# Two small reads placed second on the load queues of a fused attention and mixer kernel

## The chip, the cores and the metric

The kernel runs on one core of one Trainium2 chip. The metric is the device time of one execution in microseconds (us). Engines are named as in the profile: PE (TensorE, matmuls), PEld (its weight loads), DVE (VectorE), ACT (ScalarE), POOL (GpSimd) and SP (SyncE, which here only issues transfers). Transfers run on the core's 16 DMA engines; SP and ACT each have a queue of their own to them, and a transfer of either brings sixteen completion counts in the trace.

## The reference: what is computed

Input x has 2048 rows (tokens) of 640 bf16 numbers. Two branches work on it and a gate mixes them:

```
g = sigmoid((x * gate_w).sum(-1))
a = linear_attention(x, wqkv) @ wo      # q, k, v = x @ wqkv; 32 heads of 20; phi(q), phi(k);
                                        # kv = phi(k)^T v, z = sum phi(k); o = phi(q) kv / (phi(q) z)
h  = gelu(layernorm(x) @ w1); x1 = x + shifted(h) @ w2
b  = x1 + gelu(layernorm(x1) @ w3) @ w4
out = g * a + (1 - g) * b
```

phi(t) is t + 1 where t is positive and exp(t) elsewhere, plus 1e-6. wqkv is 640 x 1920: columns 0 to 640 are wq, the next 640 wk, the last wv.

## The kernel before

The tokens are cut into 16 tiles of 128 rows, and the 640 input columns into 5 slices of 128, so a product with wq is five matmuls that add up in one PSUM bank. All of x, q, k and the activations stay in on-chip memory. The work runs in stages: q and k of every tile (to about 54 us), then the sums over tokens that the attention needs and the first layernorm (to 78 us), w1 and w2, w3, and at the end w4 together with the attention's output, tile by tile, with the gate and the store.

What matters here is the first 10 us. All loads are issued at the start, in the order in which L716 to L739 write them, on two queues. `load_x(t)` (L702) loads x tile t, 128 rows of 1,280 bytes, on SP's queue. `load_wq(k, queue)` (L705) loads slice k of wq, its first 512 columns: 128 rows of 1,024 bytes that lie 3,840 bytes apart. `load_wk` (L708) does the same for wk, in the same 3,840-byte rows. The last 128 columns of wq come in a load of their own (L729). By queue the order is:

- SP: x tile 0, x tile 1, wq slice 2, x tile 2, wk slices 0 and 2, x tile 3, wk slice 4, x tile 4, and then turns of x tiles and further loads;
- ACT: wq slices 0, 1, 3 and 4, wk slices 1 and 3, the rest of wq;
- POOL: the gate's weights, 1,280 bytes (L734).

All of these are recorded on one line of the helper, L285. The turns (`x_turn`, L711, L281 in the profile) turn x tiles 3 to 15 from rows to columns by DMA. Tiles 0, 1 and 2 are turned on PE instead (`t_x`, L798; the transposes have L637), copied from PSUM to xT by DVE (L691) and used at once.

PE begins with matmuls on constants (`warmup`, L904) that fill the time until x tile 0 is there. `q_three` (L949) then writes the order of the first q products by hand, as pairs (tile, slice), where (1, None) and (2, None) are the transposes of that tile:

```
order = [(0, 0), (1, None), (0, 1), (1, 0), (1, 1), (0, 2), (1, 2), (0, 3), (1, 3), (2, None), (0, 4), (1, 4),
         (2, 0), (2, 1), (2, 2), (2, 3), (2, 4)]
```

The products are recorded on L942 (`stream`). `k_two` (L958) follows with k of tiles 0 and 1. `k_out` (L954) evacuates a k tile and lets ACT square the x tile into a buffer that nothing reads, `junk`, for the row sums.

Later work isn't in a fixed order: `_Items.run` (L336) picks the next piece of work by times from a clock of its own (`simulate`, L232), which counts 0.5 us for an issue and a fixed rate for bytes. Waits are worked out from the buffers: an instruction that writes what another has written waits for it (`_collect`, L122), and every transfer has a semaphore. `emit` (L296) lets POOL wait for all load semaphores at the end of its program.

Of the kernel before, what the change touches and what calls it, by code (L numbers as in the profile page):

```python
# [11 lines left out]
D = 640  # L12
# [404 lines left out]
def _build(nc, A_x, A_wqkv, A_wo, B_w1, B_w2, B_w3, B_w4, gate_w, out, dbg=None, stop=None):  # L417
    sch = _Sched(nc)
# [65 lines left out]
    junk = pa.alloc("junk", [128, 1, D], BF16)  # L484
# [94 lines left out]
    def dve(fn, reads, writes, cost=None):  # L579
        if cost is None:  # L580
            n = nfree(writes[0])
            cost = 65.0 + n / 0.96
        return sch.op("dve", fn, reads, writes, cost=cost)
# [113 lines left out]
    x2 = A_x[0]  # L697

    def dma_in(out_ap, in_ap, key, **kw):
        return sch.dma("sp", out_ap, in_ap, key, **kw)  # L700

    def load_x(t):  # L702
        dma_in(x_tok[:, t, :], x2[128 * t:128 * (t + 1), :], "x%d" % t)

    def load_wq(k, queue):  # L705
        sch.dma(queue, wq[:, k, 0:512], A_wqkv[128 * k:128 * (k + 1), 0:512], "wq%d" % k)
# [7 lines left out]
    gwr = xn[:, 1, 0:128]  # L714
    dve(lambda e: e.memset(gwr, 0.0), [], [gwr])
    load_x(0)  # L716
    load_wq(0, "act")
    load_x(1)
    load_wq(1, "act")
    load_wq(2, "sp")  # L720
# [647 lines left out]
    for t in range(NT):  # L1368
        c = t // 4
# [94 lines left out]
def bass_gated_mix__linear_attn_block__mixer_s_mlp__prompt_kernel(  # L1464
    nc, A_x, A_wqkv, A_wo, B_x, B_w1, B_w2, B_w3, B_w4, gate_w, out
):
    assert tuple(A_x.shape) == (1, S, D) and tuple(out.shape) == (1, S, D)
    assert tuple(A_wqkv.shape) == (D, 3 * D) and tuple(A_wo.shape) == (D, D)
    assert tuple(B_w1.shape) == (D, D) and tuple(B_w2.shape) == (D, D)
    assert tuple(B_w3.shape) == (D, F) and tuple(B_w4.shape) == (F, D) and tuple(gate_w.shape) == (D,)  # L1470
    _build(nc, A_x, A_wqkv, A_wo, B_w1, B_w2, B_w3, B_w4, gate_w, out)
# [28 lines left out]
```

## Time and profile before

| what | value |
|---|---|
| three runs | 259.14, 259.16 and 259.90 us; median 259.16 |
| the profiled execution | 259.62 us, of which its span (first to last instruction) 258.4 |
| PE busy | 253.2 us, 98% of the span |
| DVE, ACT, POOL busy | 145.6, 107.0, 90.2 us |
| granted PE clock | 1.00 |
| x tile 0: issue, landing | 0.79, 3.65 us |
| x tile 1: issue, landing | 1.26, 4.33 us |
| wq slice 2: issue, landing | 1.71, 6.17 us |
| wq slice 3: issue, landing | 1.72, 6.37 us |
| x tile 2: issue, landing | 2.18, 7.93 us |
| wq slice 4: issue, landing | 2.20, 8.12 us |

Times of instructions count from the start of the span. A transfer's landing is the moment at which the last of its sixteen completion counts (one from each DMA engine) arrives. In rows of the timeline the columns are the start, the length, the engine, the line, the operation and its output and inputs; what stands in brackets is the idle time of the engine just before, and what ended it. In lists of waits the columns are who waited for whom, the sum in us, the number of waits and the longest. In tables by stage each engine has its busy time and, in brackets, how many instructions; then come the granted clock, the busy share of the DMA engines and GB/s.

### The profile page before, as it was taken

To read this page: it belongs to the slowest core of one execution; us is meant where nothing else is said; L and a number is where in the kernel's file an instruction comes from. 1 tells how busy PE (TensorE), PEld (TensorE's weight loads), DVE (VectorE), ACT (ScalarE), POOL (GpSimd) and SP (SyncE) were. 2 spreads that over 40 slices of the span, in tenths; PEclk is the share of its full clock that TensorE was granted. 3 is DMA by queue.
4 is the path that set the end of the run, shared out by engine and by line. 5 is a ranking of instruction groups with operands and counts; after the bars stand their busy time and mean duration, and the time that the engine had idled before them with its cause. 6 is when DMAs were issued, how large, how long until landed. Compare 5 with 4: busy or idle time off the path is not lost.

```text
span 258.4 us, 3579 instructions
## 1 busy us (share of the span) xinstructions
PE 253.2 (98%) x1392; PEld 110.9 (43%) x1242; DVE 145.6 (56%) x290; ACT 107.0 (41%) x219; POOL 90.2 (35%) x146
## 2 busy tenths in 40 slices
PE   8899999999999999999999999999999999999997
PEld 4333333344444333334444444444444444444444
DVE  2588888899962995489999803759200033200033
ACT  1396776751356757665655600003520100253000
POOL 5012299967772143758918001223000022300000
DMA  6777799555843599462565400032100032200002
GB/s 189 221 176 182 155 142 220 157 125 119 111 102 72 103 321 387 95 103 51 127 104 128 102 10 20 0 127 50 28 0 0 20 23 101 101 1 3 0 20 102
DMA packets 57825, 26.48 MB, mean 103 GB/s; under 512 B 49188, under 2 KB 56397, under 8 KB 57808
## 3 DMA queue, kind: packets, MB, share of 16 engines
q1 hardware_dynamic: 54976, 21.87, 36.1%
q0 software_dynamic: 1168, 3.28, 4.9%
q10 hardware_dynamic: 1664, 1.11, 1.4%
q8 instruction: 10, 0.16, 0.3%
q14 instruction: 7, 0.06, 0.1%
HBM read 12.04 MB, written 2.62 MB: 57 GB/s over the span
## 4 chain that ended last, share of the span: by engine, by line
PE 95%; DMA 2%; issue 1%; SPq 0%; DVE 0%
PE ps L606 37%; PE ps L1237 30%; PE ps L625 13%; PE ps L831 7%; PE ps L614 4%; DMA x_tok<-in_A_x_dram 2%; PE ps L942 1%; PE ps L1283 1%; PE ps L1143 1%; SPq L285 0%; PE ps L1029 0%; DVE Mt L691 0%; PE ps L637 0%; PE ps L1055 0%; DVE x_tok L665 0%
## 5 line engine op out<-in xcount | busy, mean ns | idle before, releaser
L606 PE MATMUL ps<-xnT,w 128*128 128x512 bf16 x352 | 79.9, 379 | 0.5 <-issue 0.2
L665 DVE SCALAR_TENSOR_TENSOR x_tok<-ps,stg,abx 128x512 bf16<-128x512 f32 (+2 forms) x17 | 12.2, 719 | 78.4 <-PE ps L1237 78.3
L682 ACT ACTIVATE h2T<-ps 128x512 bf16<-128x512 f32 x52 | 30.7, 596 | 59.8 <-PE ps L606 59.8
L606 PEld LDWEIGHTS ps<-xnT,w 128*128 128x128 bf16 x360 | 34.6, 98 | 41.5 <-issue 2.1
L1237 PE MATMUL ps<-w,h2T 128*128 128x512 bf16 (+2 forms) x218 | 45.9, 366 | 0.3 <-issue 0.2
L648 POOL TENSOR_SCALAR xn<-x_tok,st 128x640 bf16<-128x640 bf16 x32 | 34.2, 1076 | 25.8 <-DMA xnT<-xn 25.3
L648 POOL TENSOR_SCALAR abx<-x_tok,stg 128x640 f32<-128x640 bf16 (+1 forms) x16 | 14.8, 934 | 72.1 <-DVE x_tok L665 72.1
L1237 PEld LDWEIGHTS ps<-w,h2T 128*128 128x128 bf16 x221 | 21.1, 98 | 24.2 <-issue 0.3
L682 ACT ACTIVATE Er<-ps 128x512 bf16<-128x512 f32 (+1 forms) x36 | 23.0, 648 | 15.5 <-PE ps L614 10.6
L681 ACT ACTIVATE junk<-x_tok 128x640 bf16<-128x640 bf16 x32 | 23.6, 738 | 3.9 <-DVE x_tok L663 3.7
L682 ACT ACTIVATE hsT<-ps 128x512 bf16<-128x512 f32 (+1 forms) x32 | 19.0, 593 | 13.5 <-PE ps L606 13.2
L625 PE MATMUL ps<-w,hsT 128*128 128x512 bf16 x76 | 22.3, 379 | 0.0
L625 PE MATMUL ps<-wkg,xT 128*128 128x512 bf16 x67 | 20.1, 379 | 0.1
L663 DVE SCALAR_TENSOR_TENSOR x_tok<-ps,x_tok 128x640 bf16<-128x640 f32 x16 | 13.1, 820 | 10.8 <-PE ps L614 10.2
L1237 PE MATMUL ps<-M_sb,pqnT 128*128 128x512 bf16 (+2 forms) x83 | 18.7, 366 | 0.1
L614 PE MATMUL ps<-wkg,xT 128*128 128x130 bf16 x80 | 17.6, 220 | 0.2
L831 PE MATMUL ps<-pk_tok,x_tok 128*128 128x512 bf16 x79 | 17.7, 379 | 0.1
L614 PE MATMUL ps<-w,hsT 128*128 128x128 bf16 x80 | 17.5, 219 | 0.2
L1172 DVE TENSOR_TENSOR pq_tok<-pq_tok,dnr 128x300 bf16<-128x300 bf16 (+1 forms) x48 | 17.1, 410 | 0.6
L648 DVE TENSOR_SCALAR Er<-Er 128x512 bf16<-128x512 bf16 (+1 forms) x36 | 12.2, 340 | 6.8 <-ACT Er L682 6.0
L606 PE MATMUL ps<-wq,xT 128*128 128x512 bf16 x64 | 15.9, 379 | 0.0
L656 DVE TENSOR_TENSOR qprod<-qprod,pk_tok 128x640 f32<-128x640 f32 x13 | 15.1, 1164 | 0.4
(90 smaller groups left out, 252.8 us busy)
## 6 DMA issues: line engine op xcount, KB each, us to landing
w<-in_B_w_dram SPq DMA_DIRECT2D x1, 2160.0 KB, 8.1
w<-in_B_w_dram SPq DMA_DIRECT2D x1, 2080.0 KB, 13.0
out_dram<-x_tok SPq DMA_DIRECT2D x3, 640.0 KB, 3.1
w<-in_B_w_dram POOLq DMA_DIRECT2D x8, 160.0 KB, 4.0
x_tok<-in_A_x_dram SPq DMA_DIRECT2D x6, 160.0 KB, 4.4
x_tok<-in_A_x_dram SPq DMA_DIRECT2D x1, 960.0 KB, 5.8
wv<-in_A_wqkv_dram POOLq DMA_DIRECT2D x1, 800.0 KB, 5.5
x_tok<-in_A_x_dram SPq DMA_DIRECT2D x1, 640.0 KB, 4.9
```

Of the source, the lines that this page charges most:

```text
L606: ins = e.matmul(out_ap, l, r, start=(i == 0), stop=(i == n - 1))
L614: return e.add_instruction(mybir.InstMatmult(name=nc.get_next_instruction_name(), engine=e.engine, ins=[e.lower_ap(r), ll], outs=[e.lower_ ...
L625: e.matmul(outs[0], l, r, start=st, stop=sp, skip_group_check=True)
L648: return engf(lambda e: e.tensor_scalar(out_ap, in_ap, s1, s2, op0, op1), rd, [out_ap], cost=cost)
L656: return engf(lambda e: e.tensor_tensor(out_ap, a, b_, op), [a, b_], [out_ap], cost=cost)
L663: return dve(lambda e: e.scalar_tensor_tensor(out_ap, in0, scalar, in1, op0, op1, accum_out=accum), rd, [out_ap, accum], cost=cost + 70.0)
L665: return dve(lambda e: e.scalar_tensor_tensor(out_ap, in0, scalar, in1, op0, op1), rd, [out_ap], cost=cost)
L681: return act(lambda e: e.activation(out_ap, in_ap, func, bias=bias, scale=scale, accum_out=accum), rd, wr, cost=cost)
L682: return act(lambda e: e.activation(out_ap, in_ap, func, bias=bias, scale=scale), rd, wr, cost=cost)
L831: ins = e.matmul(o, l, r, start=(t0 + q_ == 0), stop=(t0 + q_ == NT - 1))
L1172: dve(lambda e, o=o, i0=i0, i1=i1: e.tensor_tensor(o, i0, i1, ALU.mult), [i0, dnr[:, 1, sd, :]], [o], cost=cost)
L1237: ins = e.matmul(o, l, r, start=first and i == 0, stop=last and i == len(prs) - 1, skip_group_check=True)
```

## The change

Two reads are added, and nothing else. Behind x tile 0, SP issues a read of 64 bytes (32 columns) from every eighth row of x tile 2, sixteen rows in all, into 16 partitions of `junk`. Behind wq slice 0, ACT issues a read of 64 bytes from every eighth row of wq slices 1, 2, 3 and 4, sixteen rows of each slice, into the same partitions. Nothing uses the values: the same bytes are loaded again with their tiles and slices. In the words of the change that is 64 bytes of one row for each of the 16 DMA engines. Each read has a semaphore of its own.

```diff
     load_x(0)
+    sch.dma("sp", junk[0:16, 0, 128:160], x2[256:384:8, 0:32], "tx")
     load_wq(0, "act")
+    sch.dma("act", junk[0:16, 0, 0:128].rearrange("p (k c) -> p k c", c=32),
+            A_wqkv[128:D, 0:32].rearrange("(k e r) c -> e k r c", e=16, r=8)[:, :, 0, :], "tw")
     load_x(1)
     load_wq(1, "act")
     load_wq(2, "sp")
```

## The prediction

> **What bounds the kernel now.** The first view is the busy table: PE is busy for 253.2 us of a span of 258.4 us. So the kernel is bound by matmuls, and the only time to be had is where PE stands still. The second view is the list of waits of PE, cut to the first 10 us and then to the rest. The first 10 us hold this:
> ```profile
> PE ps L904 <- PEq L1485: 0.8, 1, 0.8
> PE ps L637 <- DMA x_tok<-in_A_x_dram: 0.7, 1, 0.7
> ```
> The first is the start of the program, before any load. Behind 10 us the list has two waits of 0.2 us and nothing else. So one wait counts, that of the transposes (L637) of x tile 2 for its load. The chain that ended last says the same, and from 8 us to the end it is almost all PE:
> ```profile
> 1.71 0.43 SPq L285
> 2.14 0.04 issue
> 2.18 5.75 DMA x_tok<-in_A_x_dram
> 7.93 0.05 issue
> 7.98 0.45 PE ps L637 x5
> ```
> Tile 2 is the fourth load on SP's queue, issued at 2.18, and lands 5.75 us later at 7.93. The timeline of PE and of its weight loads around it shows how much time stands open:
> ```profile
> 5.21 2.04 PE L942 MATMUL ps<-wq,xT 128*128 128x512 bf16 x7
> 7.98 0.45 PE L637 MATMUL ps<-ident,x_tok 128*128 128x128 bf16 x5 [0.73 <-DMA x_tok<-in_A_x_dram]
> ...
> 5.75 0.10 PEld L942 LDWEIGHTS ps<-wq,xT 128*128 128x128 bf16 x1 [0.29 <-DVE xT L691]
> 6.21 0.55 PEld L942 LDWEIGHTS ps<-wq,xT 128*128 128x128 bf16 x4 [0.36 <-DMA wq<-in_A_wqkv_dram]
> ```
> Matmuls of 512 columns overlap: two in a row start 0.216 us apart (five take 1.08 in the chain) though each lasts 0.379. The last of the seven ends at 7.25, so it starts at 6.87 and the next could start at 7.09: open until 7.98 are 0.89 us. The matmul of 5.75 could be followed at 5.97 and is followed at 6.21, when wq slice 2 is there: 0.24 us more. **The ceiling of any gain here is 0.89 + 0.24 = 1.13 us**, since behind 8 us PE runs without a gap.
>
> Why does tile 2 land late? The table by stage of the first loads (DMA share and GB/s are the last two columns) tells where its 5.75 us go:
> ```profile
> 3.00:4.00 1.00, 1.00 (x9) 0.63 (x8) 0.00 (x0) 0.00 (x0) 0.84 (x4) 1.00 1.00 323
> 4.00:5.00 1.00, 1.00 (x9) 0.69 (x8) 0.65 (x2) 0.85 (x1) 0.71 (x5) 1.00 0.72 224
> 5.00:6.00 1.00, 1.00 (x8) 0.44 (x5) 0.71 (x3) 0.43 (x1) 0.00 (x0) 1.00 0.82 236
> 6.00:7.00 1.00, 0.93 (x5) 0.31 (x4) 0.00 (x0) 0.00 (x0) 0.00 (x0) 1.00 1.03 353
> 7.00:8.00 1.00, 0.27 (x3) 0.02 (x2) 0.00 (x0) 0.00 (x0) 0.00 (x0) 1.00 1.07 383
> ```
> The loads fall from 323 to 224 GB/s while both queues are full, and recover at 6 us. In the trace's packet records nearly all 1,280-byte packets last 0.055 us; between 3.9 and 6.2 us some twenty last 0.2 to 0.69 us, in wq slices 2 to 4 and x tile 2 alone. The slices of wk, which lie in the same rows as wq, follow with none. The sixteen completion counts of tile 2, one per DMA engine, come between 5.44 and 7.93, fifteen of them by 7.00, where x tile 0's spread over 0.6 us. So rows that an engine has not touched before seem to cost it a stall, and tile 2 collects them.
>
> **The change, part by part.** *Issues.* Each of the two queues gets one more issue before its second load: by the rows of the page's own issues 0.40 to 0.46 us on SP and on ScalarE. Everything behind is issued that much later: tile 1 at 1.72 for 1.26, tile 2 at 2.65 for 2.18. Does that move a landing? From 2.3 us to 10 us data is queued, so at best nothing; at worst the whole 0.47 us. I take 0.25 for tile 1, as tile 0's packets last until about 2.8 us and tile 1's would be there some 1.03 us after issue (the lag of tile 0: issue at 0.79, first packet at 1.82), at 2.75 for 2.29; and 0 for what stands behind it. *Bytes.* 16 x 64 and 64 x 64 bytes are 5 KB; one packet on SP's ring and four on ScalarE's for each engine. The nearest row is the 256-byte packet of a transpose, 0.018 us: 5 x 0.018 = 0.09 us, inside the 0.25.
>
> *First touch.* The read of each new region is paid ahead, for all five regions, in 64-byte packets. What is it worth? At the least nothing, where the stall only changes its place. At the most all the stall: 4 to 6 us ran at 224 and 236 GB/s against 368 from 6 to 8 us (mean of 353 and 383), which loses 2 x (1 - 230/368) = 0.75 us on the mean engine, and the last engine is another 0.93 us late (7.00 to 7.93). The mean engine's 7.00 less 0.75 is 6.25; with x tile 0's spread of 0.6 us instead of tile 2's, and tile 1's 0.25, the last count comes by about 6.7. t_x(2) can't start before 7.98 - 1.13 = 6.85. So the load stops being the bound, and the gain is the ceiling less what tile 1 loses, since its transposes (PE at 4.37, landing at 4.33) have no slack: **1.13 - 0.25 = 0.88 us**. Late next are the DVE copies of xT (0.29 and 0.39 us of wait in the timeline), and wq slice 4, needed 0.32 us behind the start of the transposes of tile 2, at 7.3, and landing at 8.12 now, with fifteen counts by 7.26; it is one of the slices touched.
>
> *Edits at nothing.* ScalarE's table load moves from 4.15 to 4.6 and ends at 5.9; its first activation comes at 8.71, or 7.8. SP has nothing to do from 5.46 to 10.20, when it waits for tile 3. Both reads write junk, so ScalarE's first Square (12.91) waits for them; they are there by 5 us, and behind it stand only later activations. POOL gets two waits behind its last work. The order of later work is written by the planner from its own clock: there tile 1 moves from 0.894 to 1.000 us of load start, everything behind it by the same 0.106 us, and PE's wait for the gate row, the last in the planner's start-up, too. Equal shifts change no comparison, so order and banks stay. If they did not, any of the later 250 us could move; I give it no price but the edges of the range.
>
> *Is the gain kept?* PE has no wait for a load behind 8 us. The nearest is wk slice 0: needed at 9.66 - 0.88 = 8.78, landing at 8.71 and, of the same rows, earlier if the stall goes. xT of tile 5 lands at 19.0 for a matmul at 20.74.
>
> *Against the median.* The profiled execution took 259.62 us (span 258.4 and 1.2 around it), the median of three is 259.16, the others 259.14 and 259.90. How much of the 0.46 is this same stall I can't see. 259.62 - 0.88 = 258.74; I take the step, not the level, to the median: **259.16 - 0.88 = 258.3 us**. If the median execution stalls less than the profiled one, by the whole 0.46, the gain is 0.42 and the time 258.7.
>
> **The rivals.** *A: the stall only moves.* The touch stands in each ring ahead of tile 1 and wq slice 1, which wait for it; the later stall shrinks by as much. Tile 2 lands when it does now: 259.1 to 259.2. For it: the load of w3, alone on its queue, starts slowly although five blocks are touched in turn, and needs about 2 us:
> ```profile
> 90.50:91.50 1.00, 1.00 (x9) 0.44 (x5) 0.97 (x3) 0.98 (x3) 0.00 (x0) 1.00 0.62 59
> 91.50:92.50 1.00, 1.00 (x7) 0.31 (x5) 1.00 (x3) 0.03 (x1) 0.00 (x0) 1.00 0.77 218
> 93.50:94.50 1.00, 1.00 (x8) 0.46 (x6) 1.00 (x2) 0.28 (x2) 0.47 (x3) 1.00 1.05 429
> 97.50:98.50 1.00, 1.00 (x8) 0.35 (x4) 0.00 (x0) 0.97 (x2) 1.00 (x2) 1.00 1.06 396
> ```
> Against it: 64-byte reads hold little, and five can be open at once beside tile 0's data.
>
> *B: the stall is not first touch.* The last line above is w4, as new as w3, right behind it on the same queue, and at full rate from its start. So a slow start may belong to an idle queue, and the dip at 4 to 6 us to something else. Then the change brings only later issues: 0 to 0.47 us, 259.2 to 259.6. The Trainium skill, "HBM Reference", Latency, gives a mean access time of 0.2 us and 2 us at high load; by that rule the stalls come from load and a read ahead changes nothing. The trace disagrees as far as it goes: there are none at 383 GB/s and many at 224.
>
> *C: slower.* The touch stalls the rings and spares nothing, as 64 bytes warm only a piece of what an engine reads later (each reads eight rows). Then everything from tile 1 on is late by the stall: w3's longest first packet took 1.07 us, the 960 KB load of x at 22 us 1.51. Nothing covers it, since tile 2's wait is already open: 259.16 + 1.07 = 260.2, up to 260.7. From a stall of 0.78 us that isn't given back it shows as slower.
>
> **How the numbers follow.** A difference of 0.3%, 0.78 us, is about what a measurement of this kernel can tell from no change. The forecast, a gain of 0.4 to 1.13 us, has 0.55: 0.45 above 0.78 us, 0.10 below. A has 0.14 and B 0.13, both within 0.3%; C has 0.18. So faster 0.45, same 0.37, slower 0.18. The range runs from the ceiling, 259.16 - 1.13 = 258.0, less 0.1 for scatter, to B's end, 259.6: it leaves out C. The forecast's own range is 258.0 to 258.8.
>
> **What would show it.** Right: the stretch from 4 to 6 us at over 300 GB/s, long packets gone from wq slices 2 to 4 and tile 2, its landing before 7.1, the wait of L637 gone and tile 1 landing by 4.6. A: long packets in the small reads, tile 1 later by over 0.5 us, tile 2 as now. B: the dip unchanged and every landing up to 0.47 us late. C: tile 2 behind 8.9. The prediction fails if the typical execution has less stall than the profiled one, or if a load behind 8 us becomes a wait of PE.

## The result and the profile after

The changed kernel took 259.65 us (median of 22 runs, 259.19 to 261.63), the kernel before 259.02 us in the same comparison (22 runs, 258.3 to 259.9). The ratio is 1.0029 with a 95% interval of 1.0017 to 1.0040: slower, by 0.29% or some 0.7 us (what an unchanged kernel reads against itself is run 4 below). The forecast was 258.3 us and its range ended at 259.6, so the sign is the other one.

The profiled execution of the changed kernel took 259.44 us, with a span of 258.2. PE's waits in the first 10 us:

```profile
PE ps L907 <- PEq L1488: 0.8, 1, 0.8
PE ps L637 <- DMA x_tok<-in_A_x_dram: 0.5, 1, 0.5
```

The second looks like the wait of before (0.7 us), made shorter. It is another wait of the same line: the timeline shows for which tile. The transposes (L637) of tile 0 stand at 3.66, those of tiles 1 and 2 are these:

```profile
5.45 0.71 PE L637 MATMUL ps<-ident,x_tok 128*128 128x128 bf16 x5 [0.52 <-DMA x_tok<-in_A_x_dram]
5.96 2.00 PE L945 MATMUL ps<-wq,xT 128*128 128x512 bf16 x7
7.79 0.44 PE L637 MATMUL ps<-ident,x_tok 128*128 128x128 bf16 x5
...
9.68 0.38 PE L945 MATMUL ps<-wkg,xT 128*128 128x512 bf16 x1
```

Tile 2 (7.79) follows the matmuls without a wait, as the prediction wanted. Tile 1 now has one: it is turned at 5.45. In the kernel before that is 0.71 us earlier and without a wait:

```profile
4.74 0.63 PE L637 MATMUL ps<-ident,x_tok 128*128 128x128 bf16 x5
```

The chain that ended last runs through its load, which before ran through that of tile 2:

```profile
1.26 0.40 SPq L285
1.67 0.04 issue
1.71 3.70 DMA x_tok<-in_A_x_dram
5.41 0.05 issue
5.45 0.71 PE ps L637 x5
```

The issue at 1.26 is the small read, and tile 1's, behind it, comes at 1.71 for 1.26. Issued 0.45 us later, tile 1 lands 1.08 us later (5.41 for 4.33). The stages of the first loads (the last two columns are DMA share and GB/s):

```profile
3.00:4.00 1.00, 1.00 (x9) 0.68 (x8) 0.00 (x0) 0.00 (x0) 0.82 (x4) 1.00 0.67 159
4.00:5.00 1.00, 0.94 (x6) 0.34 (x4) 0.65 (x2) 0.38 (x1) 0.73 (x5) 1.00 0.93 292
5.00:6.00 1.00, 0.55 (x6) 0.55 (x6) 0.22 (x1) 0.90 (x1) 0.00 (x0) 1.00 1.06 338
```

The dip that stood at 4 to 6 us (224 and 236 GB/s) is gone from there and now stands at 3 to 4 us (159 for 323), one load earlier. The small reads did not pay for it: their packets took 0.011 us each, and the long packets (0.17 to 0.67 us) are now in tile 1's load, which had none.

**One number carries the comparison.** In the profiled execution of every kernel of this study the span is the start of the first k matmul (`ps<-wkg,xT`, 9.68 above) plus 248.5 us, to 0.1 us: 9.88 and 258.4 before, 9.68 and 258.2 after, 8.76 and 257.3 in the fastest. So only what comes before it decides. The reported time is 1.2 to 1.3 us above the span, so by this estimate before's median of 259.02 stands for a first k matmul at about 9.3, and after's 259.65 for one at 9.9. The profiled execution of before, with 9.88, was one of its slowest (259.62 of 258.3 to 259.9).

### The profile page after: what moved, and what is told of

The parts are those of the page before. It is cut to its first block, busy times and chain, and to the rows that moved or that the text cites. A ratio compares the mean times of both kernels' runs of the same rounds, so it can differ in the third digit from the quotient of the medians.

```text
span 258.2 us, 3583 instructions
## 1 busy us (share of the span) xinstructions
PE 253.2 (98%) x1392; PEld 110.8 (43%) x1242; DVE 145.0 (56%) x290; ACT 107.1 (41%) x219; POOL 90.7 (35%) x146
## 4 chain that ended last, share of the span: by engine, by line
PE 96%; DMA 1%; issue 1%; DVE 0%; SPq 0%
PE ps L606 37%; PE ps L1240 30%; PE ps L625 13%; PE ps L834 7%; PE ps L614 4%; PE ps L945 2%; DMA x_tok<-in_A_x_dram 1%; PE ps L1286 1%; PE ps L1146 1%; PE ps L1032 0%; PE ps L637 0%; SPq L285 0%; DVE Mt L691 0%; PE ps L1058 0%; DVE x_tok L665 0%
## 5 line engine op out<-in xcount | busy, mean ns | idle before, releaser
L663 DVE SCALAR_TENSOR_TENSOR x_tok<-ps,x_tok 128x640 bf16<-128x640 f32 x16 | 13.1, 821 | 10.7 <-PE ps L614 10.1
```

Source lines behind the costliest of these rows:

```text
L663: return dve(lambda e: e.scalar_tensor_tensor(out_ap, in0, scalar, in1, op0, op1, accum_out=accum), rd, [out_ap, accum], cost=cost + 70.0)
```

## The experiments

Each kernel ran beside the kernel before on the same chip. All keep the order of work on PE and DVE; the runs with a late issue add memsets on DVE at the start. "Lands" is the last of a load's sixteen counts.

**1. The change with small reads from rows already read**

```diff
-    sch.dma("sp", junk[0:16, 0, 128:160], x2[256:384:8, 0:32], "tx")
+    sch.dma("sp", junk[0:16, 0, 128:160], x2[0:128:8, 0:32], "tx")
-            A_wqkv[128:D, 0:32]...
+            A_wqkv[0:128, 0:128]...        # as many bytes, of slice 0
```

> The change, with its two small reads taken from rows that the loads ahead of them have just read (x tile 0, wq slice 0) and not from new ones: the same issues, the same 80 packets of 64 bytes, no new region touched. Theory 1 (first touch: the small reads pay the stall of new rows ahead of x tile 1): x tile 1 lands by 4.8 us and not at 5.41, x tile 2 at 7.5 to 8.4, the dip of the loads stays at 4 to 6 us; time 259.0 to 259.5. Theory 2 (the dip comes when the gate's small read of the POOL queue gets its turn, which the change moves ahead): as the change, tile 1 at 5.2 to 5.6, dip at 3 to 4 us. Theory 3 (a small transfer between two large ones empties the queue, whatever rows it reads): also as the change, 259.4 to 259.9.

Measured: 259.87 us, ratio 1.0031 (1.0013 to 1.0049). x tile 1 lands at 6.02. The loss is the change's, with nothing touched ahead: which rows the small reads name doesn't matter to it.

**2. Before, with all first loads from the same rows**

```diff
-        dma_in(x_tok[:, t, :], x2[128 * t:128 * (t + 1), :], "x%d" % t)
+        s_ = 0 if t < 3 else t
+        dma_in(x_tok[:, t, :], x2[128 * s_:128 * (s_ + 1), :], "x%d" % t)
-        sch.dma(queue, wq[:, k, 0:512], A_wqkv[128 * k:128 * (k + 1), 0:512], "wq%d" % k)
+        sch.dma(queue, wq[:, k, 0:512], A_wqkv[0:128, 0:512], "wq%d" % k)    # load_wk likewise
```

> The kernel before, with x tiles 1 and 2 read from the rows of tile 0 and with all slices of wq and wk read from the rows of slice 0: as many loads, packets and bytes, but no new rows behind the first load of each queue until x tile 3 (this computes with wrong values). Theory 1 (first touch): the dip at 4 to 6 us goes, x tile 2 lands by 6.8 us, time 0.4 to 1.0 us below before. Theories 2 and 3: the dip stays where it is, x tile 2 at 7 to 8 us, time as before.

Measured: 259.19 us, 0.9998 (0.9986 to 1.0010), with 294 and 291 GB/s at 4 to 6 us and single packets of up to 1.28 us, though the rows were those of the first loads. With run 1 this ends first touch as the cause of the dip.

**3. No gate read (POOL's queue), before and with the change**

```diff
-    sch.dma("pool", xn[0:KD, 1, 0:128], gate_w.rearrange("(k p) -> k p", p=128), "gw")
```

> The kernel before, without the read of the gate's weights on POOL's queue (they stay zero, so this leaves out the gate's sums). Theory 1 (first touch) and theory 3 (the small transfers themselves): the dip at 4 to 6 us stays, x tile 2 lands at 7 to 8 us, time within 0.4 us of before. Theory 2 (the gate's read makes the dip): 4 to 6 us at over 320 GB/s, x tile 2 by 6.8 us, time 0.4 to 1.0 us below before.

> The change, without the read of the gate's weights (they stay zero). Theory 1 and theory 3: as the change, x tile 1 lands at 5.2 to 5.6 us, dip at 3 to 4 us, time 259.4 to 259.9. Theory 2: tile 1 lands by 4.8 us, no dip, x tile 2 by 7 us, time 258.0 to 258.6.

Measured: 259.36 us, 1.0013 (0.9994 to 1.0031), without the read in the kernel before, and the dip stays (279 and 265 GB/s). 259.89 us, 1.0042 (1.0020 to 1.0063), in the changed one: the loss is all there. The small transfer on the third queue is not it.

**4. The kernel before, unchanged**

> The kernel before, unchanged, as a kernel of its own: what no change reads as, and a second trace of it. Its x tile 2 landed at 7.93 us in the first trace, in an execution 0.5 us above the median of 35. If that execution was an unlucky one, tile 2 lands here by 7.3 us and the ratio is within 0.998 to 1.002.

Measured: 259.45 us, 1.0013 (0.9999 to 1.0028). So a ratio of 1.0013, or of 0.9987, reads as no change here. Its trace has 297 and 287 GB/s at 4 to 6 us, x tile 2 at 7.54 and the first k matmul at 9.57. PE waits there for wq slice 2 (0.9 us) and not for tile 2. The dip of 224 and 236 from which the prediction was worked out, and the wait for tile 2, belong to one execution.

**5. Before, with tile 1 and wq slice 1 issued late, and no small reads**

```diff
-    load_x(1)
-    load_wq(1, "act")
+    for _ in range(2):
+        late = dve(lambda e: e.memset(junk[:, 0, :], 0.0), [], [junk[:, 0, :]], cost=230.0)
+    sch.dma("sp", x_tok[:, 1, :], x2[128:256, :], "x1", deps=[late])
+    sch.dma("act", wq[:, 1, 0:512], A_wqkv[128:256, 0:512], "wq1", deps=[late])
```

> The kernel before, with no small reads, but with x tile 1 and wq slice 1 issued 0.45 us later: they wait for two DVE memsets of junk that end about there. Theory 4 (it is the later issue: the data queues run empty behind x tile 0, and a queue that starts anew has slow first packets): x tile 1 lands at 5.2 to 6.0 us, the loads drop below 200 GB/s between 3 and 4 us, time 259.4 to 259.9. Theory 3 (the small transfer itself upsets what follows): tile 1 lands by 4.8 us, time 259.0 to 259.4.

Measured: 259.76 us, 1.0040 (1.0019 to 1.0060). The two are issued at 1.81, 0.1 us later than in the change, and land at 5.97 and 6.16. Its wait of PE for tile 1, and its stages:

```profile
PE ps L637 <- DMA x_tok<-in_A_x_dram: 1.3, 1, 1.3
```

```profile
3.00:4.00 1.00, 1.00 (x9) 0.69 (x8) 0.00 (x0) 0.00 (x0) 0.82 (x4) 1.00 0.78 105
4.00:5.00 1.00, 0.69 (x6) 0.30 (x4) 0.65 (x2) 0.25 (x1) 0.73 (x5) 1.00 0.88 255
5.00:6.00 1.00, 0.00 (x0) 0.00 (x0) 0.00 (x0) 1.00 (x1) 0.00 (x0) 1.00 1.06 368
```

**The whole loss without any small read**, and the dip in the change's place, deeper (105 GB/s). PE does nothing from 5 to 6 us. So the later issue costs, not the transfer that took the place.

**6. The small reads elsewhere in the queues**

Third (behind x tile 1 and wq slice 1), and behind all first loads:

```diff
     load_x(1)
+    sch.dma("sp", junk[0:16, 0, 128:160], x2[256:384:8, 0:32], "tx")
     load_wq(1, "act")
+    sch.dma("act", junk[0:16, 0, 0:128]..., A_wqkv[128:D, 0:32]..., "tw")
```

> The change, with both small reads behind x tile 1 and wq slice 1 and not ahead of them, so that more data is queued ahead when they come. Theory 4: x tile 1 lands at 4.2 to 4.6 as before, the queues don't run empty, x tile 2 at 7 to 8, time 258.9 to 259.4. Theory 3: what follows the reads is upset, wq slice 2 lands by over 0.7 us later than before (6.2), x tile 2 at 8 to 9, time 259.5 to 260.3.

> The change, with both small reads behind all first loads (on SP's queue behind x tile 4, on ACT's behind the rest of wq). Theory 4: no load is issued later, so the time is as before, 258.8 to 259.4, ratio 0.998 to 1.002, and x tile 1 lands at 4.2 to 4.6. Theory 3: the reads themselves cost, over 1.002.

Measured: third 259.48 us, 1.0023 (1.0007 to 1.0038). Tile 1 lands at 4.59, and the dip moves with the reads to 4 to 5 us (164 GB/s). Last 259.12 us, 1.0018 (1.0001 to 1.0035). The medians fall the further back the reads stand, but the intervals overlap, and neither of these two can be told from run 4's 1.0013: the reads' bytes and packets cost nothing that shows. With the reads last the first loads are issued as before, and its trace has 308 and 335 GB/s at 4 to 6 us, no wait of PE for a load, and the first k matmul at 9.38 all the same; run 10 says why.

**7. One part of the change alone, and one queue late alone**

```diff
     load_x(0)
+    sch.dma("sp", junk[0:16, 0, 128:160], x2[256:384:8, 0:32], "tx")     # x read only
```

```diff
     load_wq(0, "act")
+    sch.dma("act", junk[0:16, 0, 0:128]..., A_wqkv[128:D, 0:32]..., "tw")    # wq read only
```

```diff
-    load_x(1)
+    for _ in range(2):
+        late = dve(lambda e: e.memset(junk[:, 0, :], 0.0), [], [junk[:, 0, :]], cost=230.0)
+    sch.dma("sp", x_tok[:, 1, :], x2[128:256, :], "x1", deps=[late])     # tile 1 late only
```

> Of the change only the read of x tile 2 on SP's queue. Theory 4: x tile 1 is still issued 0.45 us late, but ACT's queue goes on with wq slice 1 and hides the gap in part: tile 1 at 4.6 to 5.2 us, time 259.1 to 259.5. Theory 3: one small transfer for each engine is enough, tile 1 at 5.2 to 6.0, time 259.4 to 259.9.

> Of the change only the read of the wq slices, on ACT's queue. Theory 4 (a load issued after the first data moves, at about 1.7 us, starts slowly once what was issued ahead of it is used up): x tile 1 keeps its issue at 1.26 and lands at 4.0 to 4.5 us, wq slice 1 is issued at 1.72 and lands at 5.0 to 6.0 and is what PE waits for; x tile 2 at 6.5 to 7.8; time 259.0 to 259.8. Theory 3 (the small transfer itself): tile 1 is late too, at over 4.8.

> The kernel before, with no small reads, with x tile 1 alone issued 0.45 us later (it waits for two DVE memsets of junk), and all of SP's queue behind it. It is to the run with the x read alone what the late issue of both was to the change. Theory 4: as that run, x tile 1 at 5.8 to 6.5 us, x tile 2 at 8 to 8.8, time 260.2 to 262. Theory 3: tile 1 by 4.8, time 259.0 to 259.5.

Measured: 261.42 us, 1.0087 (1.0055 to 1.0119); 260.52 us, 1.0070 (1.0043 to 1.0096); 260.89 us, 1.0071 (1.0045 to 1.0098). Each half is worse than the whole, which the forecasts of the first two had not (at most 259.9 and 259.8 us). In the two on SP's queue tile 1 lands at 6.24 and 6.80; with the read on ACT's it lands at 4.22, and wq slice 1, now issued at 1.72, at 6.43, for which PE waits 1.6 us. One queue that is late seems to fall behind the other's later loads. Tile 1 late by memsets does what the x read does, without any read. Part of the 261.42 is the clock: four of its seven executions had a mean granted clock of 0.993. Part of tile 1 late alone is PE's pace (run 10 for both).

**8. More bytes issued before the first data**

The loads of wq put together in another way, with x tile 2 as SP's third issue; no small reads:

```diff
-    load_wq(1, "act")
-    load_wq(2, "sp")
-    load_wq(3, "act")
+    sch.dma("act", wq[:, 1:5, 0:512], A_wqkv[128:640, 0:512].rearrange("(k p) f -> p k f", p=128), "wq1")
...
-    load_wq(4, "act")
```

The other two take slices 1+2 and then 3+4 as ACT's second and third, and slices 0+1 and then 2 to 4 as its first and second.

> The kernel before, with wq slices 1 to 4 in one load of 512 KB, second on ACT's queue (issued at 1.24), and x tile 2 third on SP's queue (1.71). Theory 4: more data is issued before the first moves, the rate stays over 320 GB/s from 3 to 6 us, x tile 2 lands by 6.9; but slice 1 comes with slice 4 at 5.4 to 6.2 and PE waits for it; time 258.4 to 259.0. If the dip is a matter of time or of bytes and not of issues, it is at 4 to 6 us as before and the time is 259.0 to 259.8.

> The kernel before, with wq slices 1 and 2 in one load, second on ACT's queue, slices 3 and 4 in one behind it, and x tile 2 third on SP's. Theory 4: the first two issues of each queue carry 720 KB and not 576, so the dip comes later and is shorter: x tile 2 by 7.0, slices 1 and 2 at 4.9 to 5.4 where slice 1 alone is needed at 5.2; time 258.2 to 258.9, below both kernels. If the dip doesn't hang on issues: as before.

> The kernel before, with wq slices 0 and 1 in one load, first on ACT's queue, slices 2 to 4 in one, second, and x tile 2 third on SP's. In all runs so far the span is 248.5 us behind the first k matmul, so only the first 10 us count. Theory 4: as with slices 1 to 4 in one there is no dip from 3 to 5 us, and PE doesn't wait for slice 1: first k matmul at 8.7 to 9.1, time 258.3 to 258.8, below both kernels. If long loads have stalls of their own, as with the pairs (one engine's part of slices 3 and 4 came 3 us late): 259.2 to 261.

Measured: slices 1 to 4 in one 258.99 us, 1.0003 (0.9992 to 1.0014); in pairs 260.78 us, 1.0075 (1.0048 to 1.0101); two and three 258.67 us, 0.9987 (0.9976 to 0.9998). With 960 KB in the first two issues of each queue the dip is gone. The stages of two and three:

```profile
4.00:5.00 1.00, 1.00 (x9) 0.67 (x8) 0.65 (x2) 0.66 (x1) 0.72 (x5) 1.00 1.09 388
5.00:6.00 1.00, 1.00 (x8) 0.49 (x6) 0.71 (x3) 0.00 (x0) 0.00 (x0) 1.00 1.08 386
6.00:7.00 1.00, 1.00 (x8) 0.51 (x7) 0.00 (x0) 0.00 (x0) 0.00 (x0) 1.00 1.06 389
```

PE is busy throughout, tile 2 lands at 6.09, and the first k matmul starts at 8.76:

```profile
6.88 0.44 PE L637 MATMUL ps<-ident,x_tok 128*128 128x128 bf16 x5
...
8.76 0.38 PE L939 MATMUL ps<-wkg,xT 128*128 128x512 bf16 x1
```

**In its trace this version beats both kernels**; by the median it gains 0.13%, no more than run 4's kernel is off from itself. Slices 1 to 4 in one gain nothing, as slice 1 then lands with slice 4 at 5.67 and PE waits 0.5 us for it. The pairs missed their forecast of 258.2 to 258.9: with 704 KB ahead the third issue is slow again (eight counts of slices 3+4 by 5.88, the last at 9.24), and PE waits 3.0 us for them.

**9. The small reads beside the regrouped loads**

```diff
+    sch.dma("act", wq[:, 0:2, 0:512], A_wqkv[0:256, 0:512]..., "wq0")
+    sch.dma("sp", junk[0:16, 0, 128:160], x2[256:384:8, 0:32], "tx")
+    sch.dma("act", junk[0:16, 0, 0:96]..., A_wqkv[256:D, 0:32]..., "tw")
     load_x(1)
+    sch.dma("act", wq[:, 2:5, 0:512], A_wqkv[256:640, 0:512]..., "wq2")
```

and the same with the reads third, behind both.

> The kernel with wq slices 0 and 1 in one load and 2 to 4 in one, and the change's small reads (x tile 2; slices 2 to 4) second on each queue. Theory 4: x tile 1 and slices 2 to 4 are issued at 1.7 and not at 1.25, with only 416 KB ahead of them, so the dip is back between 3 and 5 us: x tile 1 at 5 to 6 us (4.63 without the reads), first k matmul 0.4 to 1.2 us later than 8.76, time 259.0 to 260.0. If the reads only add bytes: 258.6 to 258.9.

> The same regrouped kernel with the small reads third, behind x tile 1 and slices 2 to 4, so with 960 KB queued ahead of all that they delay. Theory 4: no dip, x tile 2 issued at 2.2 and landing at 6.0 to 6.6, time 258.5 to 258.9 as without reads. If a small read costs wherever it stands ahead of needed data: x tile 2 later than 7, time over 259.1.

> The kernel of the run that regrouped wq's loads and kept the small reads second, once more: its executions fell into two groups, five at 258.9 to 259.5 us and seven at 261.3 to 262.7, and its trace was of the fastest one. Theory later issue alone: two groups differ in when x tile 1 or 2 lands, so a trace of a long one shows the first k matmul near 11.5 us (9.12 in the short one) at a clock of 1.00. Theory clock: a trace of a long one shows a granted clock below 1.00 in some slices and a first k matmul at most 1 us later. If the trace falls in the short group again, the median alone is of use: 258.9 to 262.6 us, and what makes the long group stays open.

Measured: third 258.64 us, 0.9999 (0.9979 to 1.0019): behind 960 KB the reads cost nothing that can be seen, though they also bring nothing. Second 261.44 us, 1.0073 (1.0042 to 1.0105), and once more 259.27 us, 1.0009 (0.9982 to 1.0036). Both traces were of short executions (258.85 and 258.68 us; tile 1 at 5.05 and 4.79). The forecast had the dip back between 3 and 5 us, as only 416 KB are queued ahead; neither trace has it (342 and 327 GB/s at 4 to 5 us). Seven of the first twelve executions were over 261.2 us, two of the second over 261.1, and six of these nine had a mean granted clock of 0.993 for 1.000.

**10. PE made to stand still**

```diff
-    load_x(1)
+    for _ in range(12):
+        late = dve(lambda e: e.memset(junk[:, 0, :], 0.0), [], [junk[:, 0, :]], cost=38.0)
+    sch.dma("sp", x_tok[:, 1, :], x2[128:256, :], "x1", deps=[late])
```

> Before, with x tile 1 alone held back by twelve DVE memsets instead of its place in the queue (issue at about 6.4 us by 1.34 + 11 x 0.46), no small reads. It is made to leave PE idle for more than 4 us. In every trace so far the span is the start of the first k matmul plus 248.5 us. Theory clock: the executions that are about 2 us longer, with a mean granted clock of 0.993, are those in which PE stood idle early and its clock was granted lower for a while afterwards; 0.7% of a span of 258 us is 1.8 us. Then this kernel's trace shows a granted clock below 1.00 in some slices behind 5 us, a mean of about 0.99, and a span that is longer than the first k matmul plus 248.5 us, or the first k matmul itself late by more than the load. Rival: PE's clock has nothing to do with its idle time; then every slice shows 1.00 and the span is the first k matmul plus 248.5 us. The Trainium skill, 'TensorE: Matmul & The Clock Gate', Part 1, says that the clock falls to a half after an idle window of some 3.4 us that runs freely, which would be the first of the two.

Measured: 264.79 us (263.98 to 265.01, 4 runs), 1.02 (1.0164 to 1.0236). PE has one matmul between 4.4 and 8.6 us, with waits of 2.2 and 1.7 us around it. In the stages the third column from the right is the granted clock:

```profile
7.00:8.00 1.00, 0.00 (x0) 0.00 (x0) 0.00 (x0) 0.00 (x0) 0.00 (x0) 0.67 0.58 157
10.00:11.00 1.00, 1.00 (x4) 0.43 (x3) 0.00 (x0) 0.00 (x0) 0.00 (x0) 0.50 0.93 280
14.00:15.00 1.00, 1.00 (x6) 0.40 (x4) 0.97 (x3) 0.43 (x1) 0.00 (x0) 0.92 0.36 68
```

From about 7.3 to 14.2 us the clock is 0.50, and seven matmuls take 3.19 us that take 2.00 in the changed kernel. The mean is 0.987. So a PE that stands still long enough pays twice, for the wait and for some 7 us at half speed. A mean of 0.993 is half as much, 3.6 us at half speed, 1.8 us of work lost (an estimate from these figures): about the distance of the long executions. The Trainium skill, "TensorE: Matmul & The Clock Gate", Part 1, gives a free-running window of about 3.4 us, after which an idle PE gets half the clock. The trace agrees for the half, and its half speed lasts 6.8 us, two such windows; that the window's phase decides which execution is hit would fit 5 of 12 and then 1 of 12 in one kernel, and no run here shows it, as the long executions of that kernel weren't traced.

**PE's pace at the start is a second clock effect, which the clock column hides.** At first, matmuls of 512 columns follow each other 0.43 us apart, later 0.216. The change comes at about 5.1 us in the kernel before, 6.2 in the changed one, 5.2 in two and three and 6.7 with the reads last (run 6): between 3.5 and 6.7 us in all traces but one. The tables show 1.00 all the same, since a trace's record of the clock begins only at the change (at 6.17 us in the changed kernel) or is missing. With the reads last PE waits for no load, and its first seven matmuls behind tile 1's transposes take 2.40 us where the seven behind tile 2's take 1.74:

```profile
5.26 2.40 PE L945 MATMUL ps<-wq,xT 128*128 128x512 bf16 x7
7.80 1.74 PE L945 MATMUL ps<-wq,xT 128*128 128x512 bf16 x7
```

Two and three has no wait for a load either, so its 8.76 and the 9.38 here differ, as far as the traces show, by the pace alone: part of the scatter of every kernel's times is this. The one trace with a later change is tile 1 late alone (run 7). PE stood still from 4.9 to 6.85 us, and the pace stayed slow until about 9.9, with three matmuls in a stage whose clock reads 1.00 (the last line):

```profile
6.85 0.71 PE L637 MATMUL ps<-ident,x_tok 128*128 128x128 bf16 x5 [1.91 <-DMA x_tok<-in_A_x_dram]
7.35 3.04 PE L944 MATMUL ps<-wq,xT 128*128 128x512 bf16 x7
8.00:9.00 1.00, 1.00 (x3) 0.35 (x3) 0.09 (x1) 0.00 (x0) 0.00 (x0) 1.00 1.10 344
```

With the 3.8 us that run 5 needs from these transposes on, the first k matmul would have come at about 10.7 us (an estimate); it came at 12.12. So a late tile can cost more than the wait. In the changed kernel 3 of 22 executions took over 260.9 us, in the kernel before none of 22; one of the three had a mean granted clock of 0.993, and that the other two are of this kind is likely but not shown, as none of them was traced.

## Why the prediction was wrong, step by step

- **What bounds the kernel: right.** The first 10 us decide, behind them PE keeps its pace in every kernel, and the ceiling of 1.13 us was real for the execution it was read from: 9.88 less 1.13 is 8.75, and two and three (run 8), in which PE's pace changed at nearly the same time, reached 8.76.
- **"Rows that an engine has not touched before seem to cost it a stall": wrong.** Runs 1 and 2: neither the loss nor the dip asks which rows are read. The packet records were read rightly (long packets in certain loads) but for one of 0.25 us at 7.08, in a slice of wk, and what those loads had in common was taken for their rows, when it was also their time of issue.
- **"I take 0.25 for tile 1": the term that decided.** It measured 1.08 in the changed kernel, 1.64 when issued at 1.81 (run 5), outside the bound of 0.47 too. The bound took a landing to move by no more than its issue. That tile 1's transposes "have no slack" was misread besides: PE's 4.37 is the first weight load of the transposes, their matmuls begin at 4.74, and of the 1.08 us PE lost 0.71 (to 5.45). Tile 1's first packet came at 3.12, against a forecast of 2.75, and the load then ran through the dip. The prediction put that dip down to what was loaded at 4 to 6 us. It begins where the bytes issued before the first packet (1.82 us) run out: 576 KB in the kernel before, at 3.9 us by the rates; 288 KB and the reads in the changed one, at 3.1 us; 960 KB in two and three, where none follows. Moving a load behind that edge puts it into the slow stretch. That the later issue costs is shown (run 5); the edge is argued from the traces, and run 9 with 416 KB ahead, which has no dip, and the reads last with 576 KB, which has a slight one, don't fit it well.
- **"The load stops being the bound": half right.** Tile 2's wait went, and its landing is 0.36 us earlier (7.57 for 7.93), though the kernel before, unchanged, had 7.54 in run 4. Tile 1's took its place. From its transposes to the first k matmul PE needs 3.8 us at the least (6.02 to 9.83 in run 5), so a tile 1 at 5.45 allows 9.3 at best. PE's slow pace (from the start of these transposes to the second product behind them 0.83 us, for 0.55 in run 5) and slice 3, which landed at 7.30, made it 9.68.
- **"I take the step, not the level, to the median": wrong.** The profiled execution had the deep dip. A median execution of before starts k at about 9.3, so all that could be gained was 0.55 us (to 8.76), not 1.13. The prediction named this possibility (0.46 us less) and gave it too little weight. Nor is the 0.55 the loads' alone: the pace of PE moves the first k matmul by as much (9.38 for 8.76 in run 10), which no step of the prediction had.
- **The order of later work: right.** PE's and DVE's order is the same, and nothing behind 10 us moved.
- **The rivals.** A, the stall only moves, forecast tile 1 late by over 0.5 us and tile 2 as before; the trace has 1.08 us late and 0.36 us early. Its reason, stalls in the small reads, fell, and its price of nothing was too low. B denied first touch and priced "only later issues" at 0 to 0.47 us: right in the cause, 0.6 to 0.7 us measured. C's sign came true, without the touch stalls it was built on. The rule B drew on, the Trainium skill, "HBM Reference", Latency (slow accesses come with high load), does not carry it: 105 GB/s had long packets and 389 had none.

**What stays open.** Why loads issued from about 1.7 us on start slowly when little is queued ahead isn't shown: packets of 0.2 to 1.3 us are the sign, and no run looked into what the DMA engines wait for. An empty queue alone isn't enough: in run 10 tile 1, issued at 6.40 into an empty SP queue, landed 2.17 us later, against 3.70 in the changed kernel. Why one late queue costs more than two (run 7) is argued from its falling behind, not shown. Of the executions above 261 us with a clock of 1.000 two were traced: the pairs (261.39 us), where PE waits 3.0 us for a load, and tile 1 late alone (261.86), where it is the wait and PE's pace. Why the regrouped kernel with the reads second has so many long ones isn't shown: in its traces PE waits 0.2 us for a load at the most.

## What to carry to other kernels

At a kernel's start, count the bytes that each queue has issued before the first packet comes: a transfer that takes one of those places, however small, can delay the load behind it by more than twice its issue time (1.08 us for 0.45 here), and which rows it read made no difference. Putting the first needed loads into fewer, larger issues is worth a trial and no more than that: of three groupings one gained 0.13%, one nothing, and one lost 0.75%. Before working out a gain from a profiled execution, see where it stands among the runs; a stall that is deep in one execution may be less deep in the median. Read PE's pace at a kernel's start from the distance of its matmuls, as a clock of 1.00 in the table doesn't show it. A bound on a moved load should include the stretch it moves into, not the shift of its issue alone.

## What was not expected of the hardware

- A load issued 0.45 to 0.55 us later landed 1.1 to 2.5 us later (tile 1: 5.41 in the changed kernel, 5.97 in run 5, 6.80 when alone, for 4.33).
- A 64-byte packet took 0.011 us even in the stretch where 1,280-byte packets behind it took up to 0.67 us.
- One stop of PE of about 4 us early in the span (run 10) was followed by some 7 us at a granted clock of 0.50.
- Matmuls of 512 columns came 0.43 us apart, for 0.216 later, up to 3.5 to 6.7 us into the span (9.9 once), with 1.00 in the clock column.
